# Making the second half's token operands plane by plane during the first half, and loading them whole

## The chip, the cores and the metric

The kernel runs on one core of one Trainium2 chip. The metric is the device time of one execution in microseconds. The engines of a core are PE (TensorE, matmuls, with PEld for the loading of its weights), DVE (VectorE), ACT (ScalarE), POOL (GpSimd) and SP (SyncE, which here only issues transfers). Sixteen DMA engines move data between DRAM and the on-chip memory.

## The reference

Two branches read the same tokens `x` (2048 tokens of 576 numbers) and are mixed by a gate per token:

```python
g = _sigmoid((x * gate_w).sum(-1, keepdims=True))
a = _A_ref(x, A_wqkv, A_w_phi, A_wo)             # linear attention, 32 heads
b = _B_ref(x, B_W_gate, B_W_up, B_W_down)
return g * a + (1 - g) * b

def _B_ref(x, W_gate, W_up, W_down):             # F = 4608
    gate = jnp.einsum("bsd,df->bsf", x, W_gate)
    up = jnp.einsum("bsd,df->bsf", x, W_up)
    gate = gate * (gate > 0)
    h = gate * up
    return jnp.einsum("bsf,fd->bsd", h, W_down)
```

The change concerns branch B, the feed-forward part; the attention comes before it in the kernel.

## The kernel before

**Numbers in two parts.** Matmuls read fp32r, a rounded form of fp32. Each operand is therefore split into a high part (a copy by ACT into an fp32r tile) and a low part (the operand minus its high part, a subtraction by DVE), and a product is the sum of high x high, high x low and low x high.

**Fewer products.** The feed-forward products are formed from 2 x 2 blocks with seven block products instead of eight. The token blocks are two halves of the 576 inputs by two groups of 512 tokens: `b11, b12, b21, b22`. The seven token operands are the four blocks or differences built from them, numbered 1 to 7. All tokens are first multiplied by the square root of (1 - g); the rows of these factors lie in DRAM in `sbd`.

**Operands.** A token operand in the on-chip memory is a tile `xo` of five planes of 128 partitions x 512 tokens: planes 0 to 2 are the high part (128, 128 and 32 inputs; of the third plane rows 32 to 63 hold the low part of the same 32 inputs), planes 3 and 4 the low parts of the first two. The pool `xo` holds three of them (operands 1, 5, 6) and `xo2` four (2, 7, 3, 4), so exactly one set of seven fits. `SEQ = (1, 5, 6, 2, 7, 3, 4)` is the order of the seven products in a unit.

**The loop.** There are 72 units, 36 for each half of the tokens (1024 tokens a half; `NC` is 36). A unit `u` is one piece of 128 hidden features; it has seven steps `j`, and `step(u, j)` writes down the work of one step: the product with operand `SEQ[j]` (seven matmuls, line 1143), the vector work that turns products into hidden values (`L1388` adds one product in bank `cx` to another; `L1330`, `L1333`, `L1338` follow), the splitting of hidden values (`L1274` high, `L1279` low), the weights of the next unit (`L874` to `L898`), and three to five matmuls of the down projection of an earlier pair of units (line 1174), whose results are added up in `L1240`, `L1245` or `L1189` or seeded into a bank again by ACT in `L1223`. Two units, an even and an odd one, make a pair.

**Order.** The whole loop stands in `in_order` for PE, DVE, ACT, POOL and SP: each engine does its instructions in the order in which `step` writes them down. A waiting instruction holds up all that stand behind it on its engine, and on SP each transfer waits in turn before it is issued.

**The second half's operands.** The generator `second_half`, held in `later_half`, makes the seven operands in full precision: in two passes of 256 tokens a group, it loads the four blocks, multiplies them with the factors (`L335`), forms the four differences (`L341`) and writes all seven to DRAM, to `xt`. It is advanced once per unit, at step 6 of units 4 and on, so its 16 DVE operations of 128 x 768 stand in units 5 to 12 and 14 to 21. In unit 33 what is left would be run, and the first two operands are loaded (`load_operand`). From unit 35 on `swap_in(u, j)` brings in the operands, each when its first-half counterpart has been used for the last time: the first two are split into high and low (`operand_high`, `operand_low`); for the other five, `load_in_place` loads the first two planes into the low planes, `load_rests` the third, `high_in_place` copies (ACT, `L856`, `L857`), `low_in_place` subtracts (DVE, `L861`) and `low_rest` does the 32 rows (POOL, `L841`). `xr` is a pool of two tiles of three planes used by both.

Of the kernel before, what the change touches and what calls it, by code (L numbers as in the profile page):

```python
# [7 lines left out]
F32 = mybir.dt.float32  # L8
F32R = mybir.dt.float32r
AF = mybir.ActivationFunctionType  # L10
# [5 lines left out]
P = 128  # L16
TB = 512
NTB = S // TB
NT = S // P
NC = F // P  # L20
# [63 lines left out]
def gated_mix_kernel(  # L84
# [24 lines left out]
    nc = tc.nc  # L109
    PSUM = bass.MemoryType.PSUM  # L110
    SUB, ADD, MULT = ALU.subtract, ALU.add, ALU.mult
    tt, pt = nc.vector.tensor_tensor, nc.gpsimd.tensor_tensor
# [3 lines left out]
    dram = ctx.enter_context(tc.tile_pool(name="dram", bufs=1, space=bass.MemoryType.DRAM))  # L116
# [1 line left out]
    att = dram.tile([D, S], F32, name="att")  # L118

    eT = dram.tile([NT * QK, NQ * P], F32, name="eT")  # L120
    xt = dram.tile([P, 2, 7, 3, TB], F32, name="xt")
    sbd = dram.tile([P, NTB, TB], F32, name="sbd")
    wbd = dram.tile([NC, P, 3, 5, P], F32, name="wbd")
    wsd = dram.tile([NC, P, 4, 5, P], F32, name="wsd")
# [172 lines left out]
    def whole(steps):  # L297
        for _ in steps:
            pass
# [16 lines left out]
    def on_all_rows(ps, dst, tb):  # L316

        for i in range(4):
            t = 4 * tb + i
            nc.tensor.transpose(ps[:, i * P:(i + 1) * P], rs[:, t:t + 1].to_broadcast([P, P]), ident)  # L320
        nc.scalar.activation(dst, ps, AF.Copy)

    def scaled_sums(f, hf, b, sb, c0, n, pieces=1):


        b11, b12, b21, b22 = b
        parts = [slice(i * n // pieces, (i + 1) * n // pieces) for i in range(pieces)]
        put = lambda i, a: nc.sync.dma_start(xt[:, hf, i - 1, :, c0:c0 + n], a)
        for i, a in enumerate(b):
            k, t = divmod(i, 2)  # L330
            nc.sync.dma_start(a, xs[:, k, :, (2 * hf + t) * TB + c0:(2 * hf + t) * TB + c0 + n])
        yield
        for i, a in enumerate(b):
            for c in parts:
                f(out=a[:, :, c], in0=a[:, :, c], in1=sb[:, i % 2, None, c].to_broadcast([P, 3, n // pieces]), op=MULT)  # L335
                yield
            if i != 1:
                put((1, 0, 2, 3)[i], a)
        for i, o, a, c in ((5, b11, b12, b11), (7, b12, b22, b12), (6, b22, b22, b11), (4, b21, b21, b22)):
            for p in parts:  # L340
                f(out=o[:, :, p], in0=a[:, :, p], in1=c[:, :, p], op=SUB)  # L341
                yield
            put(i, o)
# [108 lines left out]
    xw = AR.enter_context(tc.tile_pool(name="xw", bufs=4, **R_))  # L452
# [12 lines left out]
    first_half = iter(())  # L465
# [6 lines left out]
    with in_order(tc, nc, nc.gpsimd):  # L472
        for t in range(2, NT - 2):
            if t in (3, 6, 10):
                load_x((t + 2) // 4)
            if t == 8:
                whole(half_gates(0))
                sb = xw.tile([P, 2, TB], F32, name="sb", bufs=1)
                for i in range(2):
                    on_all_rows(pv1.tile([P, TB], F32, name="pg", tag="pv1"), sb[:, i], i)  # L480
                first_half = scaled_sums(pt, 0, [xw.tile([P, 3, TB], F32, name="xb") for _ in range(4)], sb, 0, TB, 2)
                with after(tc, nc, nc.sync, last_of(nc, nc.sync)):
                    next(first_half)
            if t == 12:
                for _ in first_half:
                    pass
                AR.close()
                pad = RS.enter_context(tc.tile_pool(name="pad", bufs=1, **R_))
                pad.tile([P, 24], F32, name="pad")
                kt_p = RS.enter_context(tc.tile_pool(name="kt_p", bufs=1, **R_))  # L490
                kt_ = kt_p.tile([P, 2 * TB], F32, name="kt")
                gT = kt_[:, TB:]
                kt = kt_[:, :NJ * QK].rearrange("p (g c) -> p g c", g=NJ)
                PP = [RS.enter_context(tc.tile_pool(name="ph0", bufs=1, **R_))]
                operands(BLOCKS[0])
                spread = kt_p.tile([4 * H, 5, P], F32R, name="spread")
                ones = raw.tile([4 * H, 5, P], F32, name="ones", tag="raw")
                nc.sync.dma_start(ones, spread_d)
                nc.gpsimd.tensor_copy(spread, ones)
                load_out_weights()  # L500
            if t >= 4:
                values(t, 0)
                bits(1)
            keys(t)
            if t >= 4:
                values(t, 1)
                bits(1)
            gate_logits(t)
            bits(1)
            for _ in query_steps(t - 2 if t < FIRST else t, (lambda: turn_two(t - 4)) if t >= 4 else lambda: None):  # L510
                pass
            if t >= 4:
                turn(t - 4, 2)
            kv_step(t - 2)
            bits(1)
            if t in (2, 3, 4, 5, 7):
                out_weights((2, 3, 4, 5, 7).index(t))
# [141 lines left out]
    t = NT - 1  # L659
# [119 lines left out]
    xr = ctx.enter_context(tc.tile_pool(name="xr", bufs=2, **L_))  # L779
# [30 lines left out]
    SEQ = (1, 5, 6, 2, 7, 3, 4)  # L810
    XR = {}

    def load_operand(hf, i, queue=nc.sync):
        if i < len(SEQ):
            XR[hf, i] = xr.tile([P, 3, TB], F32, name="xr", tag="xr")
            queue.dma_start(XR[hf, i], xt[:, hf, SEQ[i] - 1])

    def new_operand(hf, i):
        n = SEQ[i]
        o = XO[hf, n] = (xo if n in (1, 5, 6) else xo2).tile([P, 5, TB], F32R, name="xo", tag="xo")  # L820
        return o

    def operand_high(hf, i):

        a = XR[hf, i]
        o = new_operand(hf, i)
        nc.scalar.activation(o[:, 0:3], a, AF.Copy)

    def operand_low(hf, i):
        a, o = XR[hf, i], XO[hf, SEQ[i]]  # L830
        tt(out=o[:, 3:5], in0=a[:, 0:2], in1=o[:, 0:2].bitcast(F32), op=SUB)
        XR[hf, i] = a[:, 2]
        low_rest(hf, i, tt)
# [5 lines left out]
    def low_rest(hf, i, f):  # L839
        o, a = XO[hf, SEQ[i]], XR.pop((hf, i))  # L840
        f(out=o[32:64, 2], in0=a[32:64], in1=o[32:64, 2].bitcast(F32), op=SUB)  # L841

    def load_in_place(hf, i):

        o = new_operand(hf, i)
        nc.sync.dma_start(o[:, 3:5].bitcast(F32), xt[:, hf, SEQ[i] - 1, 0:2])

    def load_rests(hf, ii):
        a = xr.tile([P, 3, TB], F32, name="xr", tag="xr")
        for k, i in enumerate(ii):  # L850
            nc.sync.dma_start(a[:, k], xt[:, hf, SEQ[i] - 1, 2])
            XR[hf, i] = a[:, k]

    def high_in_place(hf, i):
        o = XO[hf, SEQ[i]]
        nc.scalar.activation(o[:, 0:2], o[:, 3:5].bitcast(F32), AF.Copy)  # L856
        nc.scalar.activation(o[:, 2], XR[hf, i], AF.Copy)  # L857

    def low_in_place(hf, i):
        o = XO[hf, SEQ[i]]  # L860
        tt(out=o[:, 3:5], in0=o[:, 3:5].bitcast(F32), in1=o[:, 0:2].bitcast(F32), op=SUB)  # L861
# [197 lines left out]
    sums_of = [raw.tile([P, 3, TB], F32, name="ac", tag="raw") for _ in range(4)]  # L1059
# [47 lines left out]
    def low(o, a):  # L1107
        tt(out=o[:, 1], in0=a, in1=o[:, 0].bitcast(F32), op=SUB)  # L1108
# [175 lines left out]

    def second_half():

        for c0 in (0, 256):
            sb = sums_of[2][:, 2].rearrange("p (b t) -> p b t", b=2)
            nc.sync.dma_start(sb, sbd[:, 2:4, c0:c0 + 256])
            xa, xb = (xr.tile([P, 2, 3, 256], F32, name="xb", tag="xr") for _ in range(2))  # L1290
            yield from scaled_sums(tt, 1, [xa[:, 0], xa[:, 1], xb[:, 0], xb[:, 1]], sb, c0, 256)

    def swap_in(u, j):

        i = j + 7 * (u - NC + 1)
        if 2 <= i < 7:
            if i in (2, 3):
                load_rests(1, (2, 3, 4) if i == 2 else (5, 6))
            load_in_place(1, i)
        if i in (2, 4):  # L1300
            operand_low(1, i // 2 - 1)
        if i in (1, 3):
            operand_high(1, i // 2)
        if 2 <= i - 5 < 7:
            low_in_place(1, i - 5)
        if 2 <= i - 4 < 7:
            high_in_place(1, i - 4)
        if 2 <= i - 5 < 7:
            low_rest(1, i - 5, pt)

    EVEN, ODD, T, LATE, PEND = {}, {}, {}, [], []
    done = []
# [60 lines left out]
    def step(u, j):  # L1373
# [22 lines left out]
        if j == 0:  # L1396
            if u > 0:
                a = gate_last(*LATE.pop())
# [85 lines left out]
        elif j == 6:  # L1484
            a = T["g2"]
# [48 lines left out]
        if u == NC + 1:  # L1534
            if j == 6:
                store_rest(0, 0)
                store_rest(0, 1)
                load_rest(1)
        if j == 6 and u < NC:
            if u >= 4:  # L1540
                next(later_half, None)
            if u == NC - 3:
                for _ in later_half:
                    pass
                load_operand(1, 0)
                load_operand(1, 1)

    later_half = second_half()
    with in_order(tc, nc, nc.tensor, nc.vector, nc.scalar, nc.gpsimd, nc.sync):
# [155 lines left out]
```

## Time and profile before

| | us |
|---|---|
| time, median of 3 runs (1560.9 to 1561.5) | 1561.07 |
| the profiled execution's own time | 1562.32 |
| its span | 1560.5 |
| PE busy | 1547.9 (99%) |
| DVE busy | 1246.6 (80%) |
| ACT busy | 803.4 (51%) |
| POOL busy | 265.1 (17%) |
| matmuls of the seven products, three forms of `cx`, `ca`, one of `cy` | 252.6, 253.1, 252.2, 126.0 |

Busy time is the time in which an engine has an instruction under way; matmuls overlap, so a PE that is busy is not yet PE at its peak, but a PE that is not busy is waiting. The span runs from the first to the last instruction. In rows of single instructions the columns are the start, the duration, the engine, the line, the operation, what it writes and reads, the shapes, the count and, in brackets, how long the engine was idle before it and what ended that. In rows by window they are the stretch, its length, the busy time and count of PE, PEld, DVE, ACT and POOL, the granted PE clock, the share of the DMA engines in use and GB/s.

### The profile page before, as it was taken

Reading aid. Unit: us, or ns where it says so; the run is one execution under the profiler, and the core shown is the slowest. Engines: PE = TensorE matmul, PEld = TensorE weight load, DVE = VectorE, ACT = ScalarE, POOL = GpSimd, SP = SyncE. Lnnn points to the kernel's source line nnn. Section 1 sums busy time; section 2 is a strip of 40 time slices with the busy share of each in tenths; the row PEclk is TensorE's granted clock in tenths of the full one; section 3 lists DMA queues with packets and bytes.
Section 4 is the critical chain, followed back from the end, with each engine's and each line's share of the span. In section 5 each row is a group of like instructions: output and inputs, shape, how many; then the busy total and the mean of one; then the engine's idle time right before and its main releaser. Section 6 shows DMA issues by size and latency. Waiting matters only on the chain.

```text
span 1560.5 us, 21012 instructions
## 1 busy us (share of the span) xinstructions
PE 1547.9 (99%) x7715; PEld 1294.2 (83%) x7715; DVE 1246.6 (80%) x1965; ACT 803.4 (51%) x1409; POOL 265.1 (17%) x405
## 2 busy tenths in 40 slices
PE   9999999999999999999999999999999999999998
PEld 9999996687888888888888887888888888888886
DVE  4998776489999999999988989676677677677676
ACT  4354335466677777777777775333333333333332
POOL 0126612212111111111111113111111111111110
PEclk9999999999999999999999999999999999999999
DMA  5364505597755585565555535634434433433432
GB/s 166 103 202 176 189 18 159 180 354 280 259 211 217 219 289 197 227 233 210 190 218 199 189 105 173 235 133 156 176 134 155 179 133 146 186 134 147 187 134 68
DMA packets 69731, 283.45 MB, mean 182 GB/s; under 512 B 7378, under 2 KB 17874, under 8 KB 60924
## 3 DMA queue, kind: packets, MB, share of 16 engines
q1 hardware_dynamic: 66412, 270.34, 47.1%
q0 software_dynamic: 2352, 10.11, 2.0%
q10 hardware_dynamic: 864, 1.65, 0.3%
q8 instruction: 61, 1.00, 0.3%
q14 instruction: 42, 0.34, 0.1%
HBM read 172.07 MB, written 108.60 MB: 180 GB/s over the span
## 4 chain that ended last, share of the span: by engine, by line
PE 94%; DVE 3%; DMA 1%; ACT 1%; issue 0%; POOL 0%; SPq 0%; DVEq 0%; POOLq 0%; ACTq 0%
PE cx L1143 28%; PE pd L1174 21%; PE ca L1143 14%; PE cy L1143 7%; PE kv L175 4%; PE pm L1174 4%; PE pk L175 3%; PE pq L175 3%; PE kv L421 1%; PE po L562 1%; PE pv L237 1%; PE ptr L379 1%; PE pw L175 1%; PE psf L259 1%; PE pw L657 1%
## 5 line engine op out<-in xcount | busy, mean ns | idle before, releaser
L1174 PE MATMUL pd<-hh,wd 128*128 128x512 f32 x980 | 381.7, 390 | 0.0
L1189 DVE TENSOR_TENSOR ac<-pd,ac 128x512 f32<-128x512 f32 x238 | 164.4, 691 | 139.5 <-PE pd L1174 139.4
L1143 PE MATMUL ca<-xo,ws 128*128 128x512 f32 x1008 | 253.1, 390 | 0.8 <-DVE xo L861 0.8
L1143 PE MATMUL cx<-xo,wb 128*128 128x512 f32 x1008 | 252.6, 390 | 0.3 <-DVE u L1388 0.3
L1143 PE MATMUL cx<-xo,ws 128*128 128x512 f32 x1008 | 252.2, 389 | 0.6 <-ACT cy L1384 0.5
L1274 ACT ACTIVATE hh<-g 128x512 fp32r<-128x512 f32 x249 | 148.3, 623 | 196.5 <-DVE g L1330 178.9
L1143 PEld LDWEIGHTS ca<-xo,ws 128*128 128x128 f32 x1008 | 189.6, 188 | 40.6 <-DVE xo L861 1.2
L1143 PEld LDWEIGHTS cx<-xo,ws 128*128 128x128 f32 x1008 | 189.0, 188 | 41.0 <-ACT cy L1384 1.3
L1143 PEld LDWEIGHTS cx<-xo,wb 128*128 128x128 f32 x1008 | 188.5, 188 | 41.5 <-DVE u L1388 2.6
L1174 PEld LDWEIGHTS pd<-hh,wd 128*128 128x128 f32 x980 | 184.2, 188 | 38.5 <-DVE pd L1245 0.3
L1174 PE MATMUL pd<-hl,wd 128*128 128x512 f32 x490 | 191.2, 390 | 2.1 <-DVE hl L1279 2.1
L1279 DVE TENSOR_TENSOR hl<-g,hh 128x512 fp32r<-128x512 f32 x249 | 174.3, 700 | 0.2 <-ACT hh L1274 0.2
L1105 ACT ACTIVATE wd<-wdr 128x384 fp32r<-128x384 f32 (+1 forms) x143 | 80.7, 566 | 114.0 <-PE pm L1174 114.0
L1143 PE MATMUL cy<-xo,wb 128*128 128x512 f32 x504 | 126.0, 389 | 0.0
L1094 POOL TENSOR_TENSOR wdr<-wdr 128x128 f32<-128x128 f32 x70 | 33.0, 472 | 486.8 <-DVE wd L1108 486.7
L1143 PEld LDWEIGHTS cy<-xo,wb 128*128 128x128 f32 x504 | 94.6, 188 | 19.7
L1174 PEld LDWEIGHTS pd<-hl,wd 128*128 128x128 f32 x490 | 92.1, 188 | 22.1 <-DVE hl L1279 3.1
L1330 DVE TENSOR_TENSOR g<-g,g 128x512 f32<-128x512 f32 x140 | 96.7, 691 | 2.4
L1345 ACT ACTIVATE g<-cx 128x512 f32<-128x512 f32 x73 | 43.6, 598 | 103.0 <-PE cx L1143 101.9
L1240 DVE TENSOR_TENSOR ac<-pd,ac 128x512 f32<-128x512 f32 x114 | 78.1, 685 | 22.6 <-PE pd L1174 21.4
L1117 POOL TENSOR_TENSOR wdr<-wdr 128x64 f32<-128x64 f32 x35 | 11.5, 328 | 479.7 <-DVE wd L1116 458.9
L1108 DVE TENSOR_TENSOR wd<-wdr,wd 128x384 fp32r<-128x384 f32 (+1 forms) x143 | 88.2, 618 | 2.1 <-ACT wd L1105 1.0
(259 smaller groups left out, 2708.9 us busy)
## 6 DMA issues: line engine op xcount, KB each, us to landing
wsd<-ws SPq DMA_DIRECT2D x34, 1280.0 KB
ws<-wsd SPq DMA_DIRECT2D x34, 1280.0 KB
wbd<-wb SPq DMA_DIRECT2D x34, 960.0 KB
wb<-wbd SPq DMA_DIRECT2D x34, 960.0 KB
wr<-wgu SPq DMA_DIRECT2D x36, 768.0 KB
wdr<-wd SPq DMA_DIRECT2D x36, 320.0 KB
wdr<-wd SPq DMA_DIRECT2D x36, 256.0 KB
eT<-et SPq DMA_DIRECT2D x10, 594.0 KB
```

Of the source, the lines that this page charges most:

```text
L175: nc.tensor.matmul(ps, w, m, start=i == 0, stop=i == len(pairs) - 1)
L1094: pt(out=a[:, 2], in0=a[:, 2], in1=a[:, 3], op=ADD)
L1105: nc.scalar.activation(o[:, 0], a, AF.Copy)
L1108: tt(out=o[:, 1], in0=a, in1=o[:, 0].bitcast(F32), op=SUB)
L1143: nc.tensor.matmul(ps, w, v, start=first and m == 0, stop=m == len(pairs) - 1, skip_group_check=True)
L1174: mm = lambda ps, w, v, a, z: nc.tensor.matmul(ps, w, v, start=a, stop=z, skip_group_check=True)
L1189: tt(out=a, in0=ps, in1=a, op=ADD)
L1240: tt(out=a, in0=ps, in1=a, op=ADD)
L1274: nc.scalar.activation(h, src, AF.Copy)
L1279: tt(out=l, in0=src, in1=h.bitcast(F32), op=SUB)
L1330: tt(out=b, in0=a, in1=b, op=SUB)
L1345: nc.scalar.activation(a, ps, AF.Copy)
```

## The change

The second half's operands are now made complete, with high and low parts, and kept in DRAM in a new tensor `xod` of five planes each. `second_half` goes through the three planes of the inputs one after another. For each plane it loads the four blocks (512 tokens wide), multiplies two and two with the factors, and then, operand by operand, forms the difference where there is one (DVE), copies the high part (ACT) at one advance, and subtracts for the low part (DVE) and stores to `xod` at the next. The generator is advanced twice per unit, at steps 3 and 6 of units 4 to 33; it has 18 yields per plane, so a plane takes nine units. Its two tiles are taken from `xr` once. `swap_in` becomes one load of 1280 KB per step of unit 35, into the tile whose first-half operand that step's product was the last to read. `scaled_sums` serves the first half alone and is otherwise the same.

```diff
-    xt = dram.tile([P, 2, 7, 3, TB], F32, name="xt")
+    xt = dram.tile([P, 7, 3, TB], F32, name="xt")
+    xod = dram.tile([P, 7, 5, TB], F32, name="xod")
...
     def second_half():
 
-        for c0 in (0, 256):
-            sb = sums_of[2][:, 2].rearrange("p (b t) -> p b t", b=2)
-            nc.sync.dma_start(sb, sbd[:, 2:4, c0:c0 + 256])
-            xa, xb = (xr.tile([P, 2, 3, 256], F32, name="xb", tag="xr") for _ in range(2))
-            yield from scaled_sums(tt, 1, [xa[:, 0], xa[:, 1], xb[:, 0], xb[:, 1]], sb, c0, 256)
+        sb = sums_of[2][:, 2]
+        ra, rb_ = (xr.tile([P, 3, TB], F32, name="xr", tag="xr") for _ in range(2))
+        b11, b12, b21, b22 = b = ra[:, 0], ra[:, 1], ra[:, 2], rb_[:, 0]
+        o = rb_[:, 1:3].bitcast(F32R)
+
+        def low(n, p, a):
+            if p < 2:
+                tt(out=o[:, 1], in0=a, in1=o[:, 0].bitcast(F32), op=SUB)
+                nc.sync.dma_start(xod[:, n - 1, p::3], o.bitcast(F32))
+            else:
+                tt(out=o[32:64, 0], in0=a[32:64], in1=o[32:64, 0].bitcast(F32), op=SUB)
+                nc.sync.dma_start(xod[:, n - 1, p], o[:, 0].bitcast(F32))
+
+        for p in range(3):
+            for i, a in enumerate(b):
+                k, t = divmod(i, 2)
+                nc.sync.dma_start(a, xs[:, k, p, (2 + t) * TB:(3 + t) * TB])
+            for t in range(2):
+                nc.sync.dma_start(sb, sbd[:, 2 + t])
+                yield
+                yield
+                for a in b[t::2]:
+                    tt(out=a, in0=a, in1=sb, op=MULT)
+            for n, r, a, c in ((1, b11, None, None), (2, b21, None, None), (3, b22, None, None), (5, b11, b12, b11),
+                               (7, b12, b22, b12), (6, b22, b22, b11), (4, b21, b21, b22)):
+                if a is not None:
+                    tt(out=r, in0=a, in1=c, op=SUB)
+                nc.scalar.activation(o[:, 0], r, AF.Copy)
+                yield
+                low(n, p, r)
+                yield
 
     def swap_in(u, j):
 
-        i = j + 7 * (u - NC + 1)
-        if 2 <= i < 7:
-            if i in (2, 3):
-                load_rests(1, (2, 3, 4) if i == 2 else (5, 6))
-            load_in_place(1, i)
-        if i in (2, 4):
-            operand_low(1, i // 2 - 1)
-        if i in (1, 3):
-            operand_high(1, i // 2)
-        if 2 <= i - 5 < 7:
-            low_in_place(1, i - 5)
-        if 2 <= i - 4 < 7:
-            high_in_place(1, i - 4)
-        if 2 <= i - 5 < 7:
-            low_rest(1, i - 5, pt)
+        if u == NC - 1:
+            o = new_operand(1, j)
+            nc.sync.dma_start(o.bitcast(F32), xod[:, SEQ[j] - 1])
...
-        if j == 6 and u < NC:
-            if u >= 4:
-                next(later_half, None)
-            if u == NC - 3:
-                for _ in later_half:
-                    pass
-                load_operand(1, 0)
-                load_operand(1, 1)
+        if j in (3, 6) and 4 <= u < NC - 2:
+            next(later_half, None)
```

More of the change, by code (lines that the diff above doesn't have):

```diff
@@ L321, in on_all_rows, with scaled_sums @@
         nc.scalar.activation(dst, ps, AF.Copy)
-    def scaled_sums(f, hf, b, sb, c0, n, pieces=1):
+    def scaled_sums(f, b, sb, pieces):
         b11, b12, b21, b22 = b
-        parts = [slice(i * n // pieces, (i + 1) * n // pieces) for i in range(pieces)]
-        put = lambda i, a: nc.sync.dma_start(xt[:, hf, i - 1, :, c0:c0 + n], a)
+        n = TB // pieces
+        parts = [slice(i * n, (i + 1) * n) for i in range(pieces)]
+        put = lambda i, a: nc.sync.dma_start(xt[:, i - 1], a)
         for i, a in enumerate(b):
             k, t = divmod(i, 2)
-            nc.sync.dma_start(a, xs[:, k, :, (2 * hf + t) * TB + c0:(2 * hf + t) * TB + c0 + n])
+            nc.sync.dma_start(a, xs[:, k, :, t * TB:(t + 1) * TB])
         yield
@@ L334, in scaled_sums @@
             for c in parts:
-                f(out=a[:, :, c], in0=a[:, :, c], in1=sb[:, i % 2, None, c].to_broadcast([P, 3, n // pieces]), op=MULT)
+                f(out=a[:, :, c], in0=a[:, :, c], in1=sb[:, i % 2, None, c].to_broadcast([P, 3, n]), op=MULT)
                 yield
@@ L480, in gated_mix_kernel @@
                     on_all_rows(pv1.tile([P, TB], F32, name="pg", tag="pv1"), sb[:, i], i)
-                first_half = scaled_sums(pt, 0, [xw.tile([P, 3, TB], F32, name="xb") for _ in range(4)], sb, 0, TB, 2)
+                first_half = scaled_sums(pt, [xw.tile([P, 3, TB], F32, name="xb") for _ in range(4)], sb, 2)
                 with after(tc, nc, nc.sync, last_of(nc, nc.sync)):
@@ L815, in load_operand @@
             XR[hf, i] = xr.tile([P, 3, TB], F32, name="xr", tag="xr")
-            queue.dma_start(XR[hf, i], xt[:, hf, SEQ[i] - 1])
+            queue.dma_start(XR[hf, i], xt[:, SEQ[i] - 1])
     def new_operand(hf, i):
@@ L845, in load_in_place @@
         o = new_operand(hf, i)
-        nc.sync.dma_start(o[:, 3:5].bitcast(F32), xt[:, hf, SEQ[i] - 1, 0:2])
+        nc.sync.dma_start(o[:, 3:5].bitcast(F32), xt[:, SEQ[i] - 1, 0:2])
     def load_rests(hf, ii):
@@ L850, in load_rests @@
         for k, i in enumerate(ii):
-            nc.sync.dma_start(a[:, k], xt[:, hf, SEQ[i] - 1, 2])
+            nc.sync.dma_start(a[:, k], xt[:, SEQ[i] - 1, 2])
             XR[hf, i] = a[:, k]
```

## The prediction

> **What bounds the kernel now.** I read the page first (shares, slices, chain), then the waits of PE, then busy time by unit of the feed-forward loop, then single instructions in two places.
>
> ```profile
> span 1560.5 us, 21012 instructions
> PE 1547.9 (99%) x7715; PEld 1294.2 (83%) x7715; DVE 1246.6 (80%) x1965; ACT 803.4 (51%) x1409; POOL 265.1 (17%) x405
> DVE  4998776489999999999988989676677677677676
> ```
>
> PE is busy 99% of the span, so a change that is not about matmuls can only win where PE stands still, and can lose wherever PE is made to stand still. DVE is the runner-up: 90% or more in slices 9 to 24, the first half of the loop. A unit is seven steps; an even one has 78 matmuls, an odd one 70. Units 34 to 37, by windows:
>
> ```profile
> 898.55:916.23 17.68, 17.68 (x79) 14.64 (x78) 17.08 (x26) 13.65 (x23) 2.37 (x4) 1.00 0.09 30
> 916.23:932.10 15.87, 15.87 (x72) 13.14 (x70) 11.23 (x18) 12.21 (x21) 2.12 (x5) 1.00 0.42 138
> 932.10:955.54 23.44, 20.43 (x79) 15.39 (x78) 23.36 (x28) 14.20 (x24) 10.99 (x9) 0.93 0.36 128
> 955.54:971.41 15.87, 15.87 (x71) 13.14 (x70) 13.55 (x23) 8.09 (x17) 2.46 (x5) 1.00 0.83 283
> ```
>
> Columns: stretch, length, busy us of PE, PEld, DVE, ACT, POOL, clock, DMA share, GB/s. Units 34, 35 and 37 run without a gap. Unit 36, the first of the second half, takes 23.44 where unit 34 with the same matmuls takes 17.68: **5.76 us are lost there**, with DVE full (23.36 of 23.44). The instructions behind it:
>
> ```profile
> 944.81 3.28 POOL L841 TENSOR_TENSOR xo<-xr,xo 32x512 fp32r<-32x512 f32 x2
> 946.87 2.30 DVE L861 TENSOR_TENSOR xo<-xo 128x1024 fp32r<-128x1024 f32 x1
> 947.00 0.50 PE L1174 MATMUL pd<-hl,wd 128*128 128x512 f32 x1 [1.91 <-DVE hl L1279]
> 949.23 2.07 PE L1143 MATMUL ca<-xo,ws 128*128 128x512 f32 x4 [0.81 <-DVE xo L861]
> 948.00:949.00 1.00, 0.42 (x2) 0.00 (x0) 1.00 (x1) 0.00 (x0) 0.10 (x1) 0.92 0.00 0
> 949.00:950.00 1.00, 0.77 (x2) 0.67 (x3) 1.00 (x3) 0.18 (x1) 0.00 (x0) 0.50 0.00 0
> 951.00:952.00 1.00, 1.00 (x4) 0.71 (x4) 1.00 (x2) 0.00 (x0) 0.00 (x0) 0.50 0.34 127
> 952.00:953.00 1.00, 1.00 (x5) 0.85 (x4) 1.00 (x3) 0.42 (x1) 0.00 (x0) 0.88 0.00 0
> L861 DVE TENSOR_TENSOR xo<-xo x9: 1210/1222/2304, 331.9 to 950.3; 128x1024 fp32r<-128x1024 f32 x9
> ```
>
> DVE makes low parts of the new operands (L861, median 1.222, one of 2.304 beside POOL's L841); PE waits 1.91 and 0.81 us for what queues there; then the granted clock (third column from the right) is 0.50 from 949 to 952, with 0.92 and 0.88 beside it: 0.08 + 1.5 + 0.12 = 1.7 us of the 5.76.
>
> **The change, part by part.**
>
> *Transition (units 35, 36).* Gone are the high parts on ACT, low parts on DVE, and L841 on POOL. Of DVE's 23.36 us in unit 36 five L861 go, at least 5 x 1.21 = 6.1, the slow ones more; 17.3 at most are left, with a slow hl among them, for 17.68 us of PE work. Bounds of the gain: 0 (another wait takes over) and 5.76 (unit 35 has nothing to lose). I take 5.8, as units 34 and 37 run gapless at such loads.
>
> *The seven loads that replace it.* Each brings 1280 KB (10 KB a partition, the shape of the ws load), 9.18 MB together, against 3.9 MB before (five of 512 and five of 256 KB). Load j may start when product j of unit 35 is done and must land before product j of unit 36.
>
> ```profile
> 990.00:995.00 5.00, 5.00 (x24) 4.14 (x23) 2.17 (x5) 1.83 (x4) 1.77 (x5) 1.00 1.01 421
> 925.00:932.00 7.00, 7.00 (x33) 5.79 (x32) 6.74 (x11) 4.65 (x10) 0.00 (x0) 1.00 0.92 305
> 988.52 0.42 SPq L912 DMA_DIRECT2D ws<-wsd  x1
> 913.51 1.75 PE L1143 MATMUL cx<-xo,wb 128*128 128x512 f32 x7
> 932.10 1.75 PE L1143 MATMUL cx<-xo,wb 128*128 128x512 f32 x7
> ```
>
> At the 421 GB/s of the wb and ws loads one takes 3.1 us; the first product of unit 35 ends at 917.8 (916.23 and seven matmuls of 0.227), and I allow 2 us to the first bytes, so the seventh lands near 919.8 + 21.8 = 941.6, plus about 1 to be seen. Unit 34's seventh product starts 15.0 after the unit (898.55 to 913.51); unit 36's would at 932.10 + 15.0 = 947.1: 4 us to spare; load 0 has 8. The cover goes at a mean of 337 GB/s: at 305 (smaller pieces) the seventh is 2.8 late. I take 0. SP has only wdr loads beside them.
>
> *First half, DVE.* The old generator put 16 DVE operations of 768 columns at step 6 of units 5 to 12 and 14 to 21. The new one runs at steps 3 and 6 of units 4 to 30: per plane (nine units) four products, four differences and seven low parts, 45 of 512 columns. What one costs is read from the tightest link I found: L1388, which must free cx before the seventh product of an even unit. Without an old operation (unit 32), and with one (from unit 5 into 6):
>
> ```profile
> 853.87 0.69 DVE L1240 TENSOR_TENSOR ac<-pd,ac 128x512 f32<-128x512 f32 x1 [0.99 <-PE pd L1174]
> 878.61 0.69 DVE L1388 TENSOR_TENSOR u<-cx,u 128x512 f32<-128x512 f32 x1
> 879.22 0.68 DVE L1279 TENSOR_TENSOR hl<-g,hh 128x512 fp32r<-128x512 f32 x1
> 879.97 1.75 PE L1143 MATMUL cx<-xo,wb 128*128 128x512 f32 x7
> 850.57 0.96 DVE L877 TENSOR_TENSOR wb<-wr,wb 128x768 fp32r<-128x768 f32 x1 [1.67 <-ACT wb L874]
>   PEld cx L1143: 2.6, 9
> 428.53 0.95 DVE L335 TENSOR_TENSOR xb<-xb,ac 128x768 f32<-128x768 f32 x1
> 429.40 0.68 DVE L1240 TENSOR_TENSOR ac<-pd,ac 128x512 f32<-128x512 f32 x1
> 442.18 0.69 DVE L1388 TENSOR_TENSOR u<-cx,u 128x512 f32<-128x512 f32 x1
> 442.94 1.87 PE L1143 MATMUL cx<-xo,wb 128*128 128x512 f32 x7
> ```
>
> Without: L1388 ends at 879.30, the product starts at 879.97, 0.67 later. With: 442.87 and 442.94, margin 0.07, and the product takes 1.87 instead of 1.75: PE already lost 0.12. The wait list of L1388 has nine such cases (PEld, 2.6 us in all): unit 1, and the eight pairs where an old operation stood in the odd unit. The operation took 0.87 of DVE's queue (428.53 to 429.40) and moved L1388 by 0.60, so 0.27 falls into gaps. DVE last waits for PE in the odd unit, at its third step (853.87, idle 0.99); from there to L1388 of the next even unit the queue is all but solid. So **what counts per pair is n, the new operations at steps 3 and 6 of the odd unit plus step 3 of the even one**. At 0.60 each (878.61 to 879.22), the loss is 0.60 n - 0.27 - 0.60 + 0.12 = 0.60 n - 0.75, nothing for n = 1.
>
> By the order of the generator's yields n is 4 for units (5,6) and (23,24); 3 for (9,10), (11,12), (15,16), (19,20), (27,28), (29,30); 2 for (13,14), (17,18), (21,22); 1 for (7,8), (25,26). Loss: 2 x 1.65 + 6 x 1.05 + 3 x 0.45 = **10.95 us**, less the 8 x 0.12 = 0.96 of old: +10.0. Bounds: -1.0 (all absorbed) and 45 x 0.69 = 31. The link's own rows are near the middle figure. The other 11 operations, low parts at step 6 of even units, cost nothing: 1.67 (850.57) and 0.99 of idle follow them, of which the old 0.87 at that place took no PE time; without it they would cost 0.6 each, 6.6.
>
> *First half, ACT and SP.* ACT gets 21 copies; those after a difference wait for DVE, and hh, the relu copy and the seed of a bank (L1223) queue behind.
>
> ```profile
> L1274 ACT ACTIVATE hh<-g 128x512 fp32r<-128x512 f32 x249 | 148.3, 623 | 196.5 <-DVE g L1330 178.9
> 876.77 0.59 ACT L1223 ACTIVATE pd<-ac 128x512 f32<-128x512 f32 x1
> 878.83 0.39 PE L1174 MATMUL pd<-hh,wd 128*128 128x512 f32 x1
> 878.64 0.33 SPq L1461 DMA_DIRECT2D wsd<-ws  x1
> 879.02 0.42 SPq L870 DMA_DIRECT2D wr<-wgu  x1
> 880.53 0.33 SPq L919 DMA_DIRECT2D wdr<-wd  x1
> ```
>
> The seed is ready at 877.36 for a matmul at 878.83, 1.47 to spare. A copy (0.62) waiting behind a late difference pushes it 1.9: 0.4 late in an n = 3 pair, inside the stall of 1.05 that follows one product later, so no more. A copy also waits for the store of the piece before (half a unit old, 512 KB, about 1.2 us of transfer behind a 1280 KB wsd): done some 4 us early. On SP there are 46 issues for 36, about 0.4 us each; a store waits for its low part and holds up the wr and wdr loads (879.02, 880.53) by 4 us, which the next unit reads a full unit later. Nothing on the path; if that cover went, ACT's first copy of a unit would be late by the excess.
>
> *Sum:* -5.8 + 10.0 = +4.2 us. The profiled execution took 1562.32 (span 1560.5), so 1566.5; against the median 1561.07, **1565.3**.
>
> *A rule against a row.*
>
> ```profile
> 375.72 1.88 PE L1143 MATMUL cx<-xo,wb 128*128 128x512 f32 x7 [0.29 <-DVE u L1388]
> ```
>
> Unit 36 shows the clock at 0.50 after waits of 1.91 and 0.81; the wait of 0.29 in unit 1 was followed by matmuls at full pace. My stalls reach 1.65, between them. The Trainium skill, "TensorE: Matmul & The Clock Gate" (Why this matters for your kernels), advises no PE-idle gaps over about 3 us and gives a whole idle window as cause; by it no stall here would trip the gate and the sum stays. The trace agrees only in part: its drop came after less than 3 us of idle.
>
> **The rivals.**
>
> *DVE absorbs it; faster.* For: PE never waited over 0.12 for the old operations. Against: they stood one to a pair, and already used the margin up. It decides if n operations move L1388 by under 0.6 in all. Time: 1561.1 - 5.8 - 1.0 = 1554.3.
>
> *Stalls trip the clock.* A drop as at 949 costs 1.7. After the two n = 4 pairs alone: 1568.7; after all eight of 1.05 or more: 1578.9. Against: half of any 3.4 us would still be busy.
>
> *The transition is not won:* the loads come late (at 305 GB/s, 2.8: 1568.1), or unit 36's loss was not the operands' (1571.1). For: DMA would run full for 22 us. Against: the 421 row, and L861 named in the wait.
>
> **How the numbers follow.** Forecast 0.58, absorbed 0.15, clock 0.12, transition not won 0.15. The likeliest alone spans 1562.5 to 1568 (0.1 us in the pitch moves it by 3). The range 1557 to 1571 leaves out the absorbed end and the far clock end. 0.2% is 3.1 us, about what a measurement tells from no change. Slower: 0.44 of the forecast, 0.12 clock, 0.11 transition: 0.67. Same: 0.14 + 0.04 + 0.02 = 0.20. Faster: the rest of the absorbed case, 0.13.
>
> **What would show it.** Unit 36 back at 17.7 with the clock at 1.00; no L861 and no POOL work there; PE waiting for L1388 in even units 6, 10, 12, 16, 20, 24, 28, 30 by 1 to 1.7 us, and none in 8 and 26; DVE solid in those pairs. Wrong if those waits are missing, if PE waits for an xo load, or if clock drops stand behind the waits.

## The result, and the profile after

The changed kernel takes 1565.98 us (median of 7 runs, 1564.57 to 1568.62) against 1561.41 us before (7 runs, 1560.88 to 1562.41): ratio 1.0031, interval 1.0019 to 1.0043, 4.6 us slower. The prediction's 1565.3 and its direction held. The profiled execution took 1565.42, its span is 1563.6.

The page of the changed kernel, the lines that answer to those of before:

```profile
span 1563.6 us, 21083 instructions
PE 1549.0 (99%) x7715; PEld 1290.6 (83%) x7715; DVE 1247.0 (80%) x1985; ACT 804.9 (51%) x1418; POOL 257.6 (16%) x400
DVE  4997776499999999999999878677677677677676
```

The shares hardly move; DVE does as much as before (1246.6), but stands at 9 without a break in slices 9 to 22, where slices 9, 21 and 22 stood at 8 before. Lines from the diff on have moved: 1143 is now 1145, 1174 is 1176, L1388 is L1404, L1223 is L1225.

**The transition.** Windows of the changed kernel's units 35 and 36, the stretch in which the seven loads run, and its last two us; columns as before:

```profile
925.27:941.13 15.86, 15.86 (x71) 13.14 (x70) 8.06 (x14) 9.00 (x19) 2.12 (x5) 1.00 0.84 336
941.13:958.81 17.68, 17.68 (x79) 14.64 (x78) 13.27 (x22) 7.66 (x14) 2.20 (x4) 1.00 0.72 294
930.00:952.00 22.00, 22.00 (x98) 18.21 (x97) 15.80 (x26) 10.52 (x21) 2.20 (x4) 1.00 0.97 407
950.00:951.00 1.00, 1.00 (x6) 0.84 (x5) 1.00 (x3) 0.04 (x1) 0.00 (x0) 1.00 0.85 338
951.00:952.00 1.00, 1.00 (x6) 0.82 (x5) 1.00 (x2) 1.00 (x2) 0.00 (x0) 1.00 0.23 78
```

Unit 36 takes 17.68 instead of 23.44, with the clock at 1.00 and DVE at 13.27 instead of 23.36: the whole 5.76 came back. DMA ran full at 407 GB/s. By the single packets in the trace, the last of the seventh load ends at 951.19, and the seventh product starts at 956.09: 4.9 us to spare.

**The first half.** The changed kernel's units 5 and 6, in windows as above:

```profile
410.69:445.83 35.14, 34.12 (x149) 27.62 (x148) 32.20 (x51) 25.20 (x44) 5.00 (x9) 1.00 0.52 199
```

Three single instructions of its unit 6 from the timeline (start, duration, engine, line; in brackets the idle time ahead and whose end ended it):

```profile
437.90 1.29 DVE L1311 TENSOR_TENSOR xr<-xr,ac 128x512 f32<-128x512 f32 x2
442.25 0.69 DVE L1404 TENSOR_TENSOR u<-cx,u 128x512 f32<-128x512 f32 x1
443.00 1.87 PE L1145 MATMUL cx<-xo,wb 128*128 128x512 f32 x7 [1.02 <-DVE u L1404]
```

Two rows of its waits by pairs of waiter and releaser (total, count, longest, us):

```profile
PE cx L1145 <- DVE u L1404: 3.8, 10, 1.0
PE pd L1176 <- ACT pd L1225: 1.6, 5, 0.4
```

The pair takes 35.14 where an undisturbed one takes 33.55. Two products (L1311) stand ahead of L1404, which ends at 442.94; PE's seventh product starts right after it, 1.02 idle. From the starts of the first products, the time of each pair over 33.55 (17.68 + 15.87):

| units | n | predicted | measured |
|---|---|---|---|
| 5, 6 | 4 | 1.65 | 1.59 |
| 7, 8 | 1 | 0 | 0 |
| 9, 10 | 3 | 1.05 | 1.01 |
| 11, 12 | 3 | 1.05 | 0.99 |
| 13, 14 | 2 | 0.45 | 0.73 |
| 15, 16 | 3 | 1.05 | 1.02 |
| 17, 18 | 2 | 0.45 | 0.44 |
| 19, 20 | 3 | 1.05 | 1.01 |
| 21, 22 | 2 | 0.45 | 0.40 |
| 23, 24 | 4 | 1.65 | 1.60 |
| 25, 26 | 1 | 0 | 0.06 |
| 27, 28 | 3 | 1.05 | 1.25 |
| 29, 30 | 3 | 1.05 | 1.25 |
| sum | | 10.95 | 11.35 |

The waits do not add up to these losses, for two reasons. Matmuls start 0.227 apart but each is shown as 0.39 long, so the first 0.16 of a wait does not count as idle; and the product after a wait takes 1.87 to 1.89 instead of 1.75. A wait therefore costs about 0.29 more than its idle time. And it is not one wait everywhere. Unit 5's seventh product, and two rows of unit 10:

```profile
424.42 1.88 PE L1145 MATMUL cx<-xo,wb 128*128 128x512 f32 x7
509.50 0.50 PE L1176 MATMUL pd<-hh,wd 128*128 128x512 f32 x1 [0.26 <-ACT pd L1225]
511.09 1.88 PE L1145 MATMUL cx<-xo,wb 128*128 128x512 f32 x7 [0.16 <-DVE u L1404]
```

In units 6 and 24 it is one wait of 1.02 for L1404. In units 10, 12, 20, 28 and 30 PE first waits 0.25 to 0.40 for a seed of a bank by ACT (L1225) and then 0.16 to 0.18 for L1404. And where two operations stand at step 3 of an odd unit (units 5, 15, 23), 0.25 of the pair's loss falls there, at the odd unit's own L1404, which ends at 424.36.

Before, the same sum is 0.90 (eight pairs of 0.09 to 0.12), and unit 36 adds 5.76. So the loop loses 11.35 - 0.90 - 5.76 = +4.7 us, which is the measured +4.6. That the two spans differ by 3.1 only is from ahead of the loop: unit 3 begins at 378.57 before and at 377.14 after, and over all the kernels profiled here, all with the same attention part, between 376.5 and 379.0.

### The profile page after: what moved, and what is told of

It reads as the page before. It is cut to its first block, busy times and chain, and to the rows that moved or that the text cites. A ratio compares the mean times of both kernels' runs of the same rounds, so it can differ in the third digit from the quotient of the medians.

```text
span 1563.6 us, 21083 instructions
## 1 busy us (share of the span) xinstructions
PE 1549.0 (99%) x7715; PEld 1290.6 (83%) x7715; DVE 1247.0 (80%) x1985; ACT 804.9 (51%) x1418; POOL 257.6 (16%) x400
## 3 DMA queue, kind: packets, MB, share of 16 engines
q10 hardware_dynamic: 864, 1.65, 0.3%
## 4 chain that ended last, share of the span: by engine, by line
PE 78%; DVE 17%; issue 2%; DMA 1%; ACT 1%; POOL 0%; SPq 0%; DVEq 0%; POOLq 0%; ACTq 0%
PE cx L1145 23%; PE pd L1176 17%; PE ca L1145 11%; PE cy L1145 5%; PE kv L176 4%; PE pk L176 3%; PE pq L176 3%; PE pm L1176 3%; DVE hl L1281 2%; DVE ac L1242 2%; DVE ws L879 1%; DVE g L1346 1%; PE kv L423 1%; PE po L564 1%; DVE ws L882 1%
```

## The experiments

Theory: an operation on DVE between its last wait for PE (third step of an odd unit) and L1404 of the next even unit makes PE wait; unit 36 is the other term; the terms add. Rivals: ACT's copies, the transfers, the sheer amount of DVE work, DMA lateness.

**e1: without the DVE operations.** In the new generator the products, differences and low parts are left out; ACT writes both planes.

```diff
-                    tt(out=a, in0=a, in1=sb, op=MULT)
-                    tt(out=r, in0=a, in1=c, op=SUB)
-                nc.scalar.activation(o[:, 0], r, AF.Copy)
+                nc.scalar.activation(o, r[:, None, :].to_broadcast([P, 2, TB]), AF.Copy)
...
-                tt(out=o[:, 1], in0=a, in1=o[:, 0].bitcast(F32), op=SUB)
-                tt(out=o[32:64, 0], in0=a[32:64], in1=o[32:64, 0].bitcast(F32), op=SUB)
```

> The changed kernel with the 45 DVE operations of the new generator left out (no products, differences or low parts; ACT writes both planes of each piece instead, 1.05 us a copy where it was 0.62), so all transfers and ACT's 21 instructions stay. Theory (the DVE operations delay L1404, once L1388, and PE waits for it): the first half loses nothing, neither the new 11.35 us nor the old 0.93, and the transition stays won: 1561.4 - 0.93 - 5.76 = 1554.7. Rival (the copies on ACT or the stores and waits on SP hold PE up): 1564 to 1566, as with the change.

Measured 1555.32 us, ratio to before 0.9958 (0.9945 to 0.9972). No unit from 3 to 37 is longer than 17.68 or 15.87. All transfers and ACT's work are still there, so neither holds PE up by itself: the whole loss needs DVE's operations. One thing differs besides: the stores no longer wait for DVE. That late stores held up other loads is not what the changed kernel shows: from 400 to 870 us its list of waits names one transfer as waited for (wbd<-wb, by ACT, 0.4 us).

**e2: without ACT's copies.**

```diff
-                nc.scalar.activation(o[:, 0], r, AF.Copy)
+                if p == 0 and n == 1:
+                    nc.scalar.activation(o[:, 0], r, AF.Copy)
```

> The changed kernel with 20 of the 21 high copies on ACT left out (the low parts are taken from one stale copy), DVE operations and transfers as they are. Theory (DVE alone): 1565.5 to 1566, the seven even units with three or four operations still 1.0 to 1.3 us long. Rival (ACT, which waits for the differences and then is late with the seeds of a bank, 1.6 us of PE waits for L1225 in the trace): 1562 to 1564.

Measured 1566.07, ratio 1.0030 (1.0019 to 1.0041), the sum over the pairs 11.46. PE's list of waits has no L1225 any more, and PE waits for L1404's counterpart instead, in all and in unit 10:

```profile
PE cx L1145 <- DVE u L1405: 7.0, 11, 1.0
511.36 1.89 PE L1145 MATMUL cx<-xo,wb 128*128 128x512 f32 x7 [0.71 <-DVE u L1405]
```

Unit 10 is 1.00 long here and 1.01 with the change. So the 1.6 us of waits for ACT in the changed kernel are not added to DVE's; they lie inside the same stall, as the prediction put it.

**e3: the same operations in other places.** None at step 3, one at step 6 of an odd unit, two at step 6 of an even one, behind L1404. A plane takes ten units and the copies stand at step 3 (the comments are added here):

```diff
+        for p in range(3):
...
+            yield
+            scaled(b11, b21)                     # even unit, step 6
+            factors(1)
+            yield
+            yield
+            scaled(b12)                          # odd unit, step 6
+            yield
+            copied(1)
+            yield
+            scaled(b22)                          # even
+            low(1, p, b11)
+            yield
+            copied(2)
+            yield
+            low(2, p, b21)                       # odd
+            yield
+            copied(3)
+            yield
+            low(3, p, b22)                       # even
+            minus_(5)
...
```

> The whole change with the same 45 DVE operations, copies, loads and stores, placed otherwise: none at step 3, one at step 6 of an odd unit, two at step 6 of an even unit, behind L1404 and ahead of DVE's idle time. Theory (place, not amount): n is 1 in every pair, so no pair is longer than 33.55, 1554.7. Rival (the amount of DVE work, or its transfers, costs PE time): near 1566, or between by the share of the work that matters.

Measured 1554.95, ratio to before 0.9957 (0.9944 to 0.9971): the whole change, 6.8 us faster than before (1561.75 beside it). Units 5 and 6 and unit 36 of this kernel:

```profile
411.05:444.60 33.55, 33.55 (x150) 27.78 (x148) 31.58 (x51) 25.13 (x44) 5.00 (x9) 1.00 0.58 210
930.49:948.16 17.67, 17.67 (x79) 14.64 (x78) 13.27 (x22) 7.66 (x14) 2.20 (x4) 1.00 0.72 294
```

DVE is busy for 31.58 us of the pair, with as many instructions (51) as in the changed kernel's 35.14, and PE has no gap. All pairs together, up to unit 34, are 0.36 too long. It is not the amount of work but where it stands.

**e4: one number.** In even units the first advance moves from step 3 to step 5, behind L1404.

```diff
-        if j in (3, 6) and 4 <= u < NC - 2:
+        if j in (3 if u % 2 else 5, 6) and 4 <= u < NC - 2:
```

> The changed kernel with one number changed: in even units the first advance stands at step 5, behind L1404, instead of step 3; odd units as they are. Theory: n is what stands in the odd unit alone, loss 0.45 for two, 1.05 for three, 0.65 for two with a 32-row operation: 5.1 in all instead of 11.35, so 1559.7. Rival (what counts is the DVE time per pair wherever it stands): 1566.

Measured 1559.53, ratio 0.9989 (0.9980 to 0.9998); the sum over the pairs is 5.35 where 5.1 was expected. Units 5 and 6:

```profile
410.52:444.51 33.99, 33.99 (x149) 27.62 (x148) 31.08 (x49) 25.13 (x44) 5.00 (x9) 1.00 0.67 248
```

The pair is 0.44 long, as two operations of the odd unit should make it, not 1.59.

**e5: the new generator with the old transition.**

```diff
     def swap_in(u, j):
-        if u == NC - 1:
-            o = new_operand(1, j)
-            nc.sync.dma_start(o.bitcast(F32), xod[:, SEQ[j] - 1])
+        i = j + 7 * (u - NC + 1)
+        if 2 <= i < 7:
+            if i in (2, 3):
+                load_rests(1, (2, 3, 4) if i == 2 else (5, 6))
+            load_in_place(1, i)
...
```

> The new generator as in the change, but the operands are brought in as before the change (two and one planes loaded, high parts on ACT, low parts on DVE, 32 rows on POOL), reading their planes from the new tensor, so that what is split there is already rounded and the numbers are not the reference's. Theory (two separate terms): unit 36 is 5.8 us longer again and the first half as with the change, 1566.0 + 5.8 = 1571.8. Rival (the whole loads themselves cost something that the old way did not, or the two parts hang together): 1566 to 1570.

Measured 1571.80, ratio 1.0068 (1.0053 to 1.0083). Unit 36:

```profile
942.95:966.11 23.16, 20.60 (x80) 14.94 (x78) 23.13 (x27) 14.20 (x24) 10.98 (x9) 0.93 0.37 135
```

5.48 us long again, clock 0.93; the pairs of the first half are as with the change. The two terms are separate and add.

**e7: before, without POOL's rows.** What made unit 36 long? The 32-row low parts on POOL are left out of the kernel before.

```diff
-        if 2 <= i - 5 < 7:
-            low_rest(1, i - 5, pt)
```

> The kernel before the change with the 32-row low parts of the second half's last five operands (POOL, L841) left out. Theory A (DVE's queue is full in unit 36 mainly since operations beside POOL's are stretched, about 4.2 us by their durations against the usual ones): unit 36 is 1 to 2 us long instead of 5.8, and the clock stays at 1.00: 1557 to 1558. Theory B (the amount of DVE work alone): 1561, unit 36 as before.

Measured 1557.20, ratio 0.9973 (0.9963 to 0.9982). Unit 36 of this kernel:

```profile
932.14:951.34 19.20, 18.63 (x79) 14.36 (x78) 19.16 (x27) 14.21 (x24) 3.96 (x4) 1.00 0.44 152
```

Its group of L861 (ns: shortest, median and longest of one):

```profile
L861 DVE TENSOR_TENSOR xo<-xo x9: 1209/1218/1478, 332.0 to 946.6; 128x1024 fp32r<-128x1024 f32 x9
```

Unit 36 is 1.52 long instead of 5.76, DVE is still full (19.16 of 19.20), L861 at most 1.478 where it was 2.304, and the clock stays up. From the unit's start to the start of L1388 (L1386 in e7), in the kernel before and in e7:

```profile
932.10:951.44 19.34, 16.34 (x63) 12.10 (x62) 19.34 (x22) 12.99 (x22) 10.99 (x9) 0.93 0.33 122
932.14:947.72 15.58, 15.29 (x66) 11.97 (x65) 15.58 (x22) 13.01 (x22) 3.96 (x4) 1.00 0.45 154
```

DVE does the same 22 instructions in 15.58 us instead of 19.34: with POOL's five rows beside them they were 3.76 us longer. The fall of the clock added less than the 1.7 that its dip is worth. Before, DVE's L1388 and PE's seventh product in unit 36:

```profile
951.44 0.68 DVE L1388 TENSOR_TENSOR u<-cx,u 128x512 f32<-128x512 f32 x1
952.79 1.78 PE L1143 MATMUL cx<-xo,wb 128*128 128x512 f32 x7
```

L1388 ends at 952.12. At full pace PE's nine matmuls from 949.23 on (0.227 each) would have been through by then, and the product would have started some 0.07 later, as in unit 6 of that kernel; it started 0.67 later, so about 0.6 is the slow clock's own. So 4.2 of the 5.76 hung on five POOL operations, through longer DVE operations and the clock. What is left, 1.5, comes with a full DVE; since one L861 (1.478) and one hl (0.89) still stand beside other POOL work, how much of it is the amount of DVE work alone is not shown. The Trainium skill, "SBUF — State Buffer" (Who interferes with whom), says that a DVE instruction with two inputs in SBUF contends with a GpSimd instruction that reads SBUF; the trace agrees as far as L861, with two such inputs, takes up to 2.304 beside L841 and at most 1.478 without it.

**e6 and e8: how much cover the loads have.** The loads are written down four, then six steps later.

```diff
-        if u == NC - 1:
-            o = new_operand(1, j)
-            nc.sync.dma_start(o.bitcast(F32), xod[:, SEQ[j] - 1])
+        i = j + 7 * (u - NC + 1) - 4
+        if 0 <= i < 7:
+            o = new_operand(1, i)
+            nc.sync.dma_start(o.bitcast(F32), xod[:, SEQ[i] - 1])
```

> The changed kernel with each of the seven whole loads issued four steps (9.1 us) later. Theory (the loads run at DMA's full rate and the last had some 4.9 us to spare: bytes end near 951.2, its product starts at 956.1): the last product comes 4.2 to 4.7 us late, the lateness growing by about 0.9 a step from the third product on, no clock drop: 1570.2 to 1570.7. Rival (ample cover): 1566. Rival (the waits trip the clock): 1572 or more.

Measured 1565.43, ratio 1.0031 (1.0018 to 1.0044): nothing lost, and my expectation was wrong. SP's own rows show why:

```profile
926.57 4.85 SPq L1326 DMA_DIRECT2D xo<-xod  x3
938.42 0.33 SPq L921 DMA_DIRECT2D wdr<-wd  x1
938.85 1.83 SPq L1326 DMA_DIRECT2D xo<-xod  x4
```

SP does not keep PE's steps. It takes the next transfer as soon as that one's own buffer is free; the first three went out as early as with the change, and only the four behind the wdr load, which waits until 938.42, came late, by about 3 us. By the packets, the last load ends at 954.58, 1.0 us ahead of the last product (955.61): of the 4.9 us to spare, 3.9 were used at no cost. With six steps (the `- 4` is `- 6`) six loads stand behind that load:

> The run with the loads written down four steps later delayed only four of them, behind the wdr load of unit 36 (issued at 938.85), and the last still landed before its product, so it tested the cover only in part. Here each load is written down six steps later: the first goes out at about 926.6 as with the change, and the other six stand behind that wdr load, from about 938.9 on. Theory (full rate, cover of about 5 us with the change): bytes start near 940.5 and one load takes 3.1 to 3.2 us, so the second lands 0.9 late, the fourth 2.2, the seventh 4.4 late (959.9 against 955.5): 1566.0 + 4.4 = 1570.4, unit 36 and the start of 37 about 4.4 us long, in waits under 1 us each, the clock at 1.00. Rival (the loads are hidden anyway): 1566. Rival (the clock falls): 1572.

Measured 1577.52, ratio 1.0104 (1.0087 to 1.0121), 7 us above the expectation. PE's rows of the timeline, then SP's:

```profile
945.65 1.86 PE L1145 MATMUL ca<-xo,ws 128*128 128x512 f32 x7 [1.09 <-DMA xo<-xod]
951.73 1.90 PE L1145 MATMUL cy<-xo,wb 128*128 128x512 f32 x7 [0.48 <-DMA xo<-xod]
954.90 1.85 PE L1145 MATMUL cx<-xo,ws 128*128 128x512 f32 x7 [0.56 <-DMA xo<-xod]
962.12 3.36 PE L1145 MATMUL ca<-xo,ws 128*128 128x512 f32 x7 [4.69 <-DMA xo<-xod]
```

```profile
955.09 0.34 SPq L1252 DMA_DIRECT2D outT<-ac  x1
955.53 0.38 SPq L1326 DMA_DIRECT2D xo<-xod  x1
```

And the window behind the longest wait (granted clock third from the right):

```profile
962.00:964.00 2.00, 1.88 (x5) 1.51 (x6) 0.00 (x0) 0.00 (x0) 0.00 (x0) 0.52 1.03 410
```

The first five behave as the rate says: counted from the start of unit 36 (941.68 here, 941.13 with the change), the second product starts 1.25 later than with the change (0.9 expected), the fourth 2.3 (2.2 expected) and the fifth 3.2. The rest is a queue again: the sixth load stood behind a store of the output (955.09) that waits for the down projection, so it went out at 955.53, PE waited 4.69, and the clock was at 0.52 after it. The lateness from the second load on shows that the cover is no more than some us; neither run measures its edge cleanly, since in neither were all the loads delayed evenly.

## Why the prediction was right

- *Transition, -5.8:* -5.76 measured. The prediction's 1.7 for the clock is the PE time spent at half pace; most of it ran while DVE held the seventh product up anyway, and about 0.6 was the clock's own (e7). Which part hung on POOL, the prediction left open; e7 gives 4.2, and 1.5 for the rest.
- *The loads, 0:* right; 4.9 us to spare against the 4 worked out, at 407 GB/s against 421. The 2 us allowed to the first bytes were more than it took: the first load was issued at 927.05, and its first packet starts at 928.01.
- *DVE in the first half, +10.95:* 11.35. The price per operation beyond the first (0.60) and the place (before L1388) held in ten of the thirteen pairs within 0.06. Three terms were mis-sized. For (13,14), 0.45 against 0.73: the 0.27 of gaps that the formula credits lies ahead of the even unit's step 3 (without an old operation, in unit 32, L1240 at 870.19 starts 0.69 after the instruction ahead of it; with one, in unit 6, it starts 0.47 after, at 433.82), and this pair has nothing in its odd unit to fall into it. For (27,28) and (29,30), 1.05 against 1.25: there the low parts are 32-row operations, which cost 0.72 on each side (below). These three miss by +0.68 together and the other ten by -0.28, so the sum is somewhat nearer than its terms.
- *The other 11 operations, 0:* right; e3 puts 30 of the 45 at that place and loses 0.36 in all.
- *ACT, nothing of its own:* right, by e2, and the lateness of the seed was called (0.4; five waits, the longest 0.4). It lies inside DVE's stall. But the sign named, a wait of 1 to 1.7 for L1388 alone in eight even units, shows in the trace only in units 6 and 24 (1.02); elsewhere ACT's seed takes a part of it, and the losses of 1 us stand in the lengths of the units.
- *The rival with the clock:* no fall in the first half; the page's PEclk is 9 throughout, after waits of up to 1.02 us. The stalls of 1.65 came in two pieces (0.25 in the odd unit, 1.34 in the even one).
- *A reading:* DVE was not at 90% or more in all of slices 9 to 24; slices 9, 21, 22 and 24 stand at 8. Nothing in the sum hangs on it.
- *The rival that DVE absorbs it:* it fell by its own condition, and e3 shows that the same work could have been absorbed, at 1555 where that rival put it at 1554.3.

## What to carry to other kernels

Where an engine off the critical path is over 90% busy, as DVE here, the price of more work on it is set by the place: find the instruction that frees what the bound engine needs, see its margin, and count only what stands between the last wait and that instruction. A row of the old, smaller work is the best gauge, since it shows both the delay per operation and how much of the margin is left. In a queue in program order, a transfer is as late as the wait of the one ahead of it, not as the step it is written in.

## What the runs showed of the hardware

Four DVE instructions of the changed kernel in a row, in its third plane:

```profile
804.94 0.69 DVE L1346 TENSOR_TENSOR g<-g,g 128x512 f32<-128x512 f32 x1
805.66 0.68 DVE L1299 TENSOR_TENSOR xr<-xr 32x512 fp32r<-32x512 f32 x1
806.38 0.69 DVE L1242 TENSOR_TENSOR ac<-pd,ac 128x512 f32<-128x512 f32 x1
806.99 0.68 DVE L1354 TENSOR_TENSOR g<-cx,g 128x512 f32<-128x512 f32 x1
```

This 32-row operation is as long as a 128-row one (0.68), but neither it nor the one ahead of it overlaps with the next: 0.72 from start to start on both sides, where the two 128-row ones behind it are 0.61 apart. It differs from its neighbours in the number of rows and in the partition at which it starts (32), and no run here separates the two. The clock fell at the end of a single wait of 4.69 us (e8) and, before the change, within a wait of 0.81 that stood close behind one of 1.91; it did not fall after 1.02. In the 3.41 us ahead of the fall before the change (at 948.83) PE was busy for 1.42; in the 3.40 ahead of 443.00 in the changed kernel, for 2.38. Where in between the clock falls was not found.
